# Exponents copied out of PSUM, one ScalarE Relu per block of w_out, GpSimd first at the shared port, first q and k loads in two parts

## The chip, the cores and the metric

The kernel runs on one core of one Trainium2 chip, as one program. The metric is the device time in microseconds, as the median of several runs; one more execution was recorded by the profiler. TensorE (PE) does the matrix products, ScalarE (ACT) the activations, VectorE (DVE) and GpSimd (POOL) elementwise work and reductions, and SyncE (SP) issues nearly all DMAs.

## The reference, cut to what matters

```python
# q, k, v: (4 batches, 8 heads, 576 positions, 64); w_in (512, 2048); w_out (2048, 512)
q_rot, k_rot = rotate(q), rotate(k)              # x*cos + swapped x*sin
scores = q_rot @ k_rot^T / sqrt(64)
attn = exp(scores - max(scores)); attn = attn / (sum(attn) + 1e-9)
x = (attn @ v), heads side by side               # 2304 tokens x 512
h = x @ w_in
g = h * tanh(softplus(h))                        # mish
out = g @ w_out
```

The weights w_in and w_out arrive as 64-bit floats; the kernel turns them into pairs of 16-bit halves (a high and a low part) with integer operations.

## The kernel before, in words

**Tiles.** Attention goes by pairs of heads (P = 0 to 15, four to a batch) and by five blocks of queries (t = 0 to 4). One step is: scores into PSUM (`psc`, L507 and L501), the negated row maximum on DVE (`mx`, L515), exp with a row sum on ACT (`e`, L517), the inverse of the sum on DVE (L526, L528). For the first batch (P below 4) the weights are then transposed on PE (L550 to L567) into `et`, copied out by ACT or DVE (L557, L558, L571 to L575), and multiplied with v (L645 to L648). For the others POOL or ACT makes the high half (`ew`, L532 or L534), DVE the low half (L538), and DMA transposes both. The multilayer part works on half a batch at a time: `h_unit` (L879, then Mish on ACT, L884), `h_split` into halves (`g`, L894 on ACT or L895 on DVE, then L898 on DVE), and `p_sub` (L915), which ends in an output.

**Rope.** Each head pair's q and k load is one DMA of 576 KB into `raw` (L405). Two multiplications by `cs` (L411) and two additions (L415), each over half of the 576 positions, follow on POOL or, in the first batch only, on DVE. A scaling of q by 0.125 on ACT closes it (L433).

**Weights.** A block's largest magnitude is found by DVE (L734, L378), crossed over the partitions by a PE transpose (L381) and a second reduction (L383), turned into an exponent (L371) and sent back to all partitions by a PE product with ones (L387); readers of the exponent read that PSUM bank. `decode` then takes each of four column blocks: ACT L775, a shift on POOL, ACT or DVE (L777 to L779), DVE L781 and L784, ACT L787, POOL L791. For w_out, `w2_decode` makes four scales at a time, one for each block of w_in: once a 128x4 `rel` (L831), and then for every block two more 128x4 operations (the two `ts` calls that make `s4`, both recorded as L371).

**Order.** The program states its operations in Python order with priorities; `Plan.order` plays them through with estimated durations and writes each engine's fixed list. Its rule for the port that DVE and POOL share: an operation whose entry has a fourth element may not start while the other engine runs one, and the two engines take turns (`turn`). ACT has two function tables, one for exp and one for Mish; a change of table costs `SWITCH` in the plan, and the plan keeps a table for at least `DWELL` ns. `SLOTS` says between which matmul groups of each half batch the attention steps go, `FRONT` how many steps go ahead of all; the `W` tables say at which step each weight block is loaded, scaled and decoded. Every engine works its list off in order and waits at each entry for what it reads.

Of the kernel before, what the change touches and what calls it, by code (L numbers as in the profile page):

```python
# [13 lines left out]
I32 = mybir.dt.int32  # L14
# [16 lines left out]
W1L = [2, 0, 1, 4]  # L31
W1S = [2, 3, 6, 7]
W1D = [5, 3, 7, 7]
VA = 4
W2L = [6, 8, 11, 9]
W2D = [10, 14, 14, 16]
PRE0 = 0
WSH = 10
FRONT = 11
TR = 107 / 128  # L40
ALPHA = 36
SLOTS = [
    [1, 8, 9, 12, 13, 17, 20, 21, 23, 27, 28, 31],
    [0, 2, 9, 10, 10, 11, 14, 15, 17, 17, 18, 19, 19, 20, 21, 25, 26, 26, 26, 31, 31],
    [8, 8],
    [5, 9, 10, 11, 12, 12, 15, 19, 20, 21, 22, 22, 22, 22, 25, 25, 26],
    [31],
    [0, 1, 2, 4, 9, 12, 12, 15, 16, 17, 18, 19, 22, 23, 23, 24, 24, 25, 25, 27, 28, 28, 30, 30],
    [],
    [1, 1, 2, 3, 4, 12, 18, 19, 21, 23, 24, 24, 24, 25, 28, 31],  # L50
]
AVL = 3
PREP = [5, 4, 0, 11]
PSH = [136, 39, 337]
ACTQ = ('out',)
QKB = 6
SWITCH = 1400
DWELL = 2251
PEN = 8
# [3 lines left out]
class Buf:  # L63


    def __init__(self, make, before=(), planned=True, of=None):
        self.planned, self.of = planned, of
        self.make, self.before, self.ops, self.state, self.ap = make, list(before), [], {}, None
        self.ring, self.slot = None, None
# [7 lines left out]
class Plan:  # L77
# [18 lines left out]
    def op(self, ways, w=(), r=(), table=None, after=()):  # L96
# [9 lines left out]
        for b, part in [x if isinstance(x, tuple) else (x, None) for x in r]:  # L106
# [23 lines left out]
    def order(self):  # L130
# [30 lines left out]
        port, turn = dict.fromkeys((DVE, POOL), 0.0), DVE  # L161
# [21 lines left out]
        while len(issued) < len(ops):  # L183
# [5 lines left out]
            for e in (PE, ACT, turn, POOL if turn == DVE else DVE, SP):  # L189
# [3 lines left out]
                while ready[e] or other:  # L193
# [49 lines left out]
                    else:  # L243
# [10 lines left out]
                        if len(ways[k]) > 3:  # L254
                            port[e], turn = end, POOL if e == DVE else DVE
# [61 lines left out]
def attention_mish_mlp(ctx: ExitStack, tc: tile.TileContext, qk, v, vflat, rope, ident_in, w_in, w_out, outT):  # L317
# [57 lines left out]
    def max_exponent(am, cols, lo, hi):  # L375
# [12 lines left out]
        return Buf(lambda: pb()[:, 0:1], planned=False, of=pb)  # L388
# [14 lines left out]
    def rope_turn(P, j, out=None):  # L403
        t = sbuf((128, 2, S), F32, "raw", 3)
        load("qk", dma_ns(128 * 2 * S * 4), lambda dma: dma(t(), qk[P][:, 2 * j:2 * j + 2]),  # L405
             w=[(t, 0), (t, 1), (t, 2), (t, 3)])
        for c in range(2):
            s = slice(c * HS, (c + 1) * HS)
# [4 lines left out]
            def add(e, s=s):  # L413
# [4 lines left out]
            op([(POOL, pool_ns(S), lambda f=mul: f(nc.gpsimd), 1), (DVE, dve_ns(S), lambda f=mul: f(nc.vector), 1)][:n],  # L418
               w=[(t, c), (t, 2 + c)], r=[cs])
            op([(POOL, pool_ns(HS), lambda f=add: f(nc.gpsimd), 1), (DVE, dve_ns(HS), lambda f=add: f(nc.vector), 1)][:n],  # L420
# [653 lines left out]
```

## Time and profile before

| what | value |
|---|---|
| median of 3 runs | 670.77 us (664.63, 670.91, 670.77) |
| the profiled execution | 662.89 us, span 661.1 us |
| mean granted TensorE clock | 0.968 |
| busy: PE, DVE, ACT, POOL | 599.6, 443.1, 455.6, 282.5 us |
| DMA | 82.50 MB, 125 GB/s over the span |
| ACT table loads | 66, of 1.283 us each |

PE is busy for 91% of the span, and the slices show where it is not: the first five, and a few after them. From about 200 us on most slices are full. A busy share is an average over stages; what bounds a stage is read from which wait ends last in it.

### The profile page before, as it was taken

Reading aid. Unit: us, or ns where it says so; the run is one execution under the profiler, and the core shown is the slowest. Engines: PE = TensorE matmul, PEld = TensorE weight load, DVE = VectorE, ACT = ScalarE, POOL = GpSimd, SP = SyncE. Lnnn points to the kernel's source line nnn. Section 1 sums busy time; section 2 is a strip of 40 time slices with the busy share of each in tenths; the row PEclk is TensorE's granted clock in tenths of the full one; section 3 lists DMA queues with packets and bytes.
Section 4 is the critical chain, followed back from the end, with each engine's and each line's share of the span. In section 5 each row is a group of like instructions: output and inputs, shape, how many; then the busy total and the mean of one; then the engine's idle time right before and its main releaser. Section 6 shows DMA issues by size and latency. Waiting matters only on the chain. (4 is left out here: it accounts for less than half of the span.)

```text
span 661.1 us, 13085 instructions
## 1 busy us (share of the span) xinstructions
PE 599.6 (91%) x5028; PEld 445.3 (67%) x5028; DVE 443.1 (67%) x961; ACT 455.6 (69%) x848; POOL 282.5 (43%) x264
## 2 busy tenths in 40 slices
PE   0576799889989998999999999999999999999997
PEld 0343455566668765678887677688877777887775
DVE  4998879998988888677776486875676576211210
ACT  2863979899889987488768776687869555623420
POOL 4795655666546876536362565460222010000000
PEclk9975978999989998999999999999999999999999
DMA  9961341452277765994667347663362376000000
GB/s 363 419 231 46 98 162 60 163 172 73 56 152 201 136 192 132 222 194 94 139 147 130 93 103 182 120 145 73 71 128 51 72 134 137 23 9 9 17 11 30
DMA packets 143534, 82.50 MB, mean 125 GB/s; under 512 B 129264, under 2 KB 133488, under 8 KB 141936
## 3 DMA queue, kind: packets, MB, share of 16 engines
q1 hardware_dynamic: 138864, 76.96, 46.9%
q10 hardware_dynamic: 4608, 4.72, 2.5%
q8 instruction: 39, 0.64, 0.4%
q14 instruction: 23, 0.19, 0.1%
HBM read 45.09 MB, written 4.72 MB: 75 GB/s over the span
## 5 line engine op out<-in xcount | busy, mean ns | idle before, releaser
L915 PE MATMUL bank<-g,w 128*128 128x256 f16 (+1 forms) x1536 | 201.9, 287 | 2.4 <-DVE g L898 1.2
L915 PEld LDWEIGHTS <-w 128*128 128x128 f16 x1536 | 146.9, 98 | 47.3 <-issue 10.5
L879 PEld LDWEIGHTS <-w 128*128 128x128 f16 x1536 | 148.8, 98 | 42.8 <-issue 6.2
L879 PE MATMUL bank<-xt,w 128*128 128x256 f16 (+1 forms) x1344 | 174.4, 286 | 2.5 <-DVE ew L575 0.8
L538 DVE SCALAR_TENSOR_TENSOR ew<-e,rs,ew 128x576 f16<-128x576 f32 x108 | 105.3, 997 | 27.8 <-POOL ew L532 18.2
L517 ACT ACTIVATE e<-psc,mx 128x576 f32<-128x576 f32 x144 | 105.7, 737 | 24.5 <-DVE mx L515 21.4
L532 POOL TENSOR_SCALAR ew<-e,rs 128x576 f16<-128x576 f32 x67 | 54.7, 824 | 157.9 <-DVE rs L528 99.7
L515 DVE TENSOR_REDUCE mx<-psc 128x1 f32<-128x576 f32 x144 | 103.4, 749 | 23.2 <-PE psc L507 19.7
L411 POOL TENSOR_TENSOR raw<-raw,cs 128x576 f32<-128x576 f32 x62 | 91.8, 1498 | 39.0 <-DMA raw<-in_qk 39.0
L898 DVE SCALAR_TENSOR_TENSOR g<-mh,cells,g 128x512 f16<-128x512 f32 (+1 forms) x64 | 58.2, 916 | 65.7 <-ACT g L894 65.7
L507 PE MATMUL psc<-qk 64*128 64x288 f32 (+1 forms) x736 | 86.9, 351 | 10.0 <-ACT e L517 7.1
L507 PEld LDWEIGHTS psc<-qk 64*128 64x128 f32 (+1 forms) x736 | 58.0, 189 | 32.3 <-ACT e L517 13.7
L884 ACT ACTIVATE mh<-bank,cells 128x256 f32<-128x256 f32 (+1 forms) x112 | 52.9, 500 | 32.3 <-PE bank L879 31.6
L791 POOL TENSOR_TENSOR w<-mr,w 128x512 f16<-128x512 f32 x30 | 35.9, 1201 | 40.7 <-ACT w L787 32.7
L534 ACT ACTIVATE ew<-e,rs 128x576 f16<-128x576 f32 x41 | 31.3, 774 | 26.6 <-DMA et<-ew 22.0
L526 DVE TENSOR_SCALAR sm<-sm 128x1 f32<-128x1 f32 x144 | 21.0, 149 | 37.0 <-ACT e L517 36.5
L894 ACT ACTIVATE g<-mh,cells 128x512 f16<-128x512 f32 (+1 forms) x55 | 42.5, 772 | 4.3 <-PE bank L915 3.3
L415 POOL TENSOR_TENSOR raw<-raw 128x288 f32<-128x288 f32 x48 | 44.6, 948 | 0.2
L517 ACT ACT_TABLE_LOAD x32 | 41.1, 1283 | 5.0 <-DVE mx L515 4.6
L884 ACT ACT_TABLE_LOAD x33 | 42.3, 1283 | 0.7
L923 ACT ACTIVATE ot<-bank,cells 128x256 f32<-128x256 f32 (+1 forms) x32 | 15.9, 496 | 37.1 <-PE bank L915 37.0
L657 PE MATMUL bank<-et,v 128*64 128x256 f16 (+1 forms) x288 | 40.8, 292 | 0.0
(104 smaller groups left out, 747.2 us busy)
## 6 DMA issues: line engine op xcount, KB each, us to landing
raw<-in_qk SPq DMA_DIRECT2D x32, 576.0 KB, 4.7
w<-in_w_in SPq DMA_DIRECT2D x4, 1024.0 KB, 12.4
stg<-in_v SPq DMA_DIRECT2D x12, 320.0 KB, 3.6
stg<-in_vflat SPq DMA_DIRECT2D x9, 384.0 KB, 3.5
w<-in_w_out SPq DMA_DIRECT2D x3, 1024.0 KB, 5.0
out_dram<-ot ACTq DMA_DIRECT2D x16, 160.0 KB, 2.4
g<-in_w_in SPq DMA_DIRECT2D x2, 1024.0 KB, 13.7
xt<-in_w_out SPq DMA_DIRECT2D x2, 1024.0 KB, 4.9
```

The source lines that it names most:

```text
L411: e.tensor_tensor(out=t()[:, :, s], in0=t()[:, :, s], in1=cs()[:, :, s], op=ALU.mult)
L415: e.tensor_tensor(out=to, in0=t()[:, 0, s], in1=t()[:, 1, s], op=ALU.add)
L507: nc.tensor.matmul(out, x[own, q], y[own, s], **kw)
L515: op((DVE, dve_ns(S), lambda: nc.vector.tensor_reduce(m(), pt()[:, :, :HS], axis=AX.XY, op=ALU.max, negate=True)), w=[m], r=[pt])
L517: op((ACT, act_ns(S, psum=True, ptr=2), lambda: nc.scalar.activation(e().rearrange("p (c s) -> p c s", c=2), pt()[:, :, :HS], AF.Exp, bias ...
L532: op([(POOL, 1.27 * S, lambda: nc.gpsimd.tensor_scalar(w()[:, c], e(), r()[:, h:h + 1], 1.0, op0=ALU.mult, op1=ALU.mult), 1), (ACT, act_ns ...
L538: op((DVE, dve_ns(S) + 61, lambda: nc.vector.scalar_tensor_tensor(out=w()[:, c], in0=e(), scalar=r()[:, h:h + 1], in1=w()[:, hc], op0=ALU. ...
L879: nc.tensor.matmul(hp(), w1()[:, wi, cc, f:f + 128], x()[:, xi, cc, q0:q0 + n], start=cc == 0 and a == 0, stop=cc == NCC - 1 and a == 2)
L884: op((ACT, act_ns(n, psum=True, ptr=1), lambda j=j, hp=hp: nc.scalar.activation(hn()[:, j, :n], hp(), AF.Mish, scale=uh())), w=[(hn, j)], ...
L894: op([(ACT, act_ns(2 * n, ptr=1), lambda: nc.scalar.activation(g()[:, 0, f, :n], hn()[:, :, :n], AF.Copy, scale=f32(gs))), (DVE, dve2_ns(2 ...
L898: op((DVE, dve_ns(2 * n) + 61, lambda: nc.vector.scalar_tensor_tensor(out=g()[:, 1, f, :n], in0=hn()[:, :, :n], scalar=f32(gs), in1=g()[:, ...
L915: nc.tensor.matmul(pp()[:, :n], w2e[e]()[:, wi, f], g()[:, gi, f % 8, :n], start=f == 0 and a == 0, stop=f == NF - 1 and a == 2)
```

## The change

- `max_exponent` now copies the exponent from the PSUM bank into an SBUF cell (one DVE COPY for each of 12 calls; 4 copies of w_in exponents that existed before are these now).
- `w2_decode`: the 128x4 `rel` and both 128x4 operations per block are gone. A 128x1 `rel`, a 128x1 bias per block, and one ACT Relu of 128x4 per block (4 in all) make the same scales.
- In the plan, POOL is always asked before DVE when the port is free; the turn-taking is gone.
- The rope constants and the loads of the first head pair come in two parts, 320 and 256 positions; for the first batch all rope work is cut at 320, the scaling of q follows each part, and the scores ask only for the part of q that they use (`QH`). The second part of q gets a later priority (`LATE`).
- `turned` takes banks only while another stays free; some duration estimates of the plan, `ALPHA`, `DWELL` (2251 to 308), `PEN`, `WSH`, the `W` tables, `PREP`, `PSH` and all of `SLOTS` are new, so that every engine's list is another.

Counted over the lists: ACT table loads 66 to 84; L894 on ACT 55 to 47 and its DVE form L895 9 to 17; L534 on ACT 41 to 34 and its POOL form L532 67 to 74; rope on DVE 2 multiplications and 3 additions to none. All matrix products are the same.

```diff
@@ -28,35 +28,38 @@
-W1L = [2, 0, 1, 4]
-W1S = [2, 3, 6, 7]
-W1D = [5, 3, 7, 7]
-VA = 4
-W2L = [6, 8, 11, 9]
-W2D = [10, 14, 14, 16]
+W1L = [0, 1, 2, 0]
+W1S = [0, 2, 2, 1]
+W1D = [6, 7, 8, 10]
+VA = 3
+W2L = [5, 3, 12, 14]
+W2D = [10, 15, 15, 17]
-WSH = 10
+WSH = 2
-ALPHA = 36
+ALPHA = 26
-    [1, 8, 9, 12, 13, 17, 20, 21, 23, 27, 28, 31],
+    [2, 8, 11, 12, 12, 18, 19, 21, 22, 23, 23, 26, 30],
...
-PREP = [5, 4, 0, 11]
-PSH = [136, 39, 337]
+LATE = 34
+PREP = [6, 4, 0, 11]
+PSH = [284, 1, 119]
+QH = [[0], [0], [0, 1], [1], [0, 1]]
+CUT = 320
-DWELL = 2251
-PEN = 8
+DWELL = 308
+PEN = 6
@@ -66,7 +69,7 @@
-        self.ring, self.slot = None, None
+        self.ring, self.slot, self.part = None, None, None
@@ -103,7 +106,7 @@
-        for b, part in [x if isinstance(x, tuple) else (x, None) for x in r]:
+        for b, part in [x if isinstance(x, tuple) else (x, x.part) for x in r]:
@@ -158,7 +161,7 @@
-        port, turn = dict.fromkeys((DVE, POOL), 0.0), DVE
+        port = dict.fromkeys((DVE, POOL), 0.0)
@@ -186,7 +189,7 @@
-            for e in (PE, ACT, turn, POOL if turn == DVE else DVE, SP):
+            for e in (PE, ACT, POOL, DVE, SP):
@@ -252,7 +255,7 @@
-                            port[e], turn = end, POOL if e == DVE else DVE
+                            port[e] = end
@@ -372,7 +375,7 @@
-    def max_exponent(am, cols, lo, hi):
+    def max_exponent(am, cols, lo, hi, out=None):
@@ -385,7 +388,10 @@
-        return Buf(lambda: pb()[:, 0:1], planned=False, of=pb)
+        got = small() if out is None else Buf(lambda: out[0]()[:, out[1]:out[1] + 1], of=out[0])
+        op((DVE, 70, lambda: nc.vector.tensor_copy(got(), pb()[:, 0:1])), w=[out or got], r=[pb])
+        got.part = out and out[1]
+        return got
@@ -400,12 +406,19 @@
-    def rope_turn(P, j, out=None):
+    def rope_turn(P, j, out=None, late=0):
-        load("qk", dma_ns(128 * 2 * S * 4), lambda dma: dma(t(), qk[P][:, 2 * j:2 * j + 2]),
-             w=[(t, 0), (t, 1), (t, 2), (t, 3)])
-        for c in range(2):
-            s = slice(c * HS, (c + 1) * HS)
+        halves = [slice(0, CUT), slice(CUT, S)] if P < NP else [slice(0, HS), slice(HS, S)]
+        if P == 0:
+            for c, s in enumerate(halves):
+                load("qk", dma_ns(256 * (s.stop - s.start) * 4), lambda dma, s=s: dma(t()[:, :, s], qk[P][:, 2 * j:2 * j + 2, s]),
+                     w=[(t, c), (t, 2 + c)])
+        else:
+            load("qk", dma_ns(128 * 2 * S * 4), lambda dma: dma(t(), qk[P][:, 2 * j:2 * j + 2]),
+                 w=[(t, 0), (t, 1), (t, 2), (t, 3)])
+        for c, s in enumerate(halves):
+            m = s.stop - s.start
+            plan.shift += late * c
@@ -415,10 +428,14 @@
-            op([(POOL, pool_ns(S), lambda f=mul: f(nc.gpsimd), 1), (DVE, dve_ns(S), lambda f=mul: f(nc.vector), 1)][:n],
-               w=[(t, c), (t, 2 + c)], r=[cs])
-            op([(POOL, pool_ns(HS), lambda f=add: f(nc.gpsimd), 1), (DVE, dve_ns(HS), lambda f=add: f(nc.vector), 1)][:n],
+            op([(POOL, pool_ns(2 * m), lambda f=mul: f(nc.gpsimd), 1), (DVE, dve_ns(2 * m), lambda f=mul: f(nc.vector), 1)][:n],
+               w=[(t, c), (t, 2 + c)], r=[(cs, c)] if P < NP else [(cs, 0), (cs, 1)])
+            op([(POOL, pool_ns(m), lambda f=add: f(nc.gpsimd), 1), (DVE, dve_ns(m), lambda f=add: f(nc.vector), 1)][:n],
+            if out is not None and j == 0:
+                op((ACT, act_ns(m), lambda s=s: nc.scalar.activation(out()[:, 0, s], out()[:, 0, s], AF.Copy, scale=0.125)),
+                   w=[(out, (0, c))])
+            plan.shift -= late * c
@@ -429,9 +446,7 @@
-            rope_turn(P, 0, z)
-            op((ACT, act_ns(S), lambda: nc.scalar.activation(z()[:, 0], z()[:, 0], AF.Copy, scale=0.125)),
-               w=[(z, (0, 0)), (z, (0, 1))])
+            rope_turn(P, 0, z, LATE)
@@ -486,7 +501,7 @@
-            terms, need, ns = (lambda: [(z()[:, 0], z()[:, 1])]), [(z, (j, c)) for j in range(2) for c in range(2)], 480
+            terms, need, ns = (lambda: [(z()[:, 0], z()[:, 1])]), [(z, (1, c)) for c in range(2)] + [(z, (0, c)) for c in QH[t]], 480
@@ -506,7 +521,7 @@
-        op((PE, 2 * ns + 100, fn), w=pts, r=need)
+        op((PE, 2 * ns + 300, fn), w=pts, r=need)
@@ -542,7 +557,7 @@
-            pt = bank()
+            pt = bank(1)
@@ -556,7 +571,7 @@
-        pt = bank()
+        pt = bank(1)
@@ -661,7 +676,7 @@
-            op((PE, 5 * pe_ns(3, n) + 220, fn), w=[po], r=[(V, 0), (V, 1)] + [(ET, x) for x in need])
+            op((PE, 5 * pe_ns(3, n) + 170, fn), w=[po], r=[(V, 0), (V, 1)] + [(ET, x) for x in need])
@@ -803,11 +818,10 @@
-        e = max_exponent(*st["w1", fq].amax(), 113.0, 142.0)
-        sc["w1s", fq], sc["w1u", fq] = pow2(e, -1, 143), pow2(e, 8, -897)
-        op((DVE, 70, lambda: nc.vector.tensor_copy(sc["w1e"]()[:, fq:fq + 1], e())), w=[(sc["w1e"], fq)], r=[e])
+        e = max_exponent(*st["w1", fq].amax(), 113.0, 142.0, (sc["w1e"], fq))
+        sc["w1s", fq], sc["w1u", fq] = pow2(e, -1, 143), pow2(e, 8, -897)
@@ -826,13 +840,13 @@
-            big, rel, all4 = small(), small((128, 4)), [(sc["w1e"], fq) for fq in range(4)]
+            big, all4 = small(), [(sc["w1e"], fq) for fq in range(4)]
-            tiny(rel, [big, *all4], lambda: nc.vector.tensor_scalar(
-                rel(), sc["w1e"](), big(), 143.0, op0=ALU.subtract, op1=ALU.add))
-            sc["w1rel"], sc["w1umax"] = rel, pow2(big, 8, -897)
-        s4 = ts(small((128, 4)), sc["w1rel"], e, 0.0, ALU.subtract, ALU.max)
-        s4 = ts(small((128, 4), I32), s4, BIT, None, ALU.mult)
+            sc["w1rel"], sc["w1umax"] = ts(small(), big, -1.0, 143.0, ALU.mult, ALU.add), pow2(big, 8, -897)
+        bias = ts(small(), sc["w1rel"], e, BIT, ALU.subtract, ALU.mult)
+        s4 = small((128, 4), I32)
+        op((ACT, 150, lambda: nc.scalar.activation(s4(), sc["w1e"](), AF.Relu, bias=bias(), scale=BIT)),
+           w=[s4], r=[bias] + [(sc["w1e"], fq) for fq in range(4)])
@@ -992,7 +1006,8 @@
-        op((SP, dma_ns(128 * 2 * S * 4), lambda: nc.sync.dma_start(cs(), rope)), w=[cs])
+        for c, s in enumerate((slice(0, CUT), slice(CUT, S))):
+            op((SP, dma_ns(256 * (s.stop - s.start) * 4), lambda s=s: nc.sync.dma_start(cs()[:, :, s], rope[:, :, s])), w=[(cs, c)])
```

**The first loads (SP) and POOL's first work.** SP before; `w_69` and the `g` tiles are homes of w_in blocks, the `raw` rows are k and q of pair 0, then of pair 1:

```order
L995 DMA cs<-in_rope 128x1152
L405 DMA raw<-in_qk 128x1152
L721 DMA w_69<-in_w_in 128x1024 x2
L405 DMA raw<-in_qk 128x1152
L996 DMA ident<-in_ident 128x128
L405 DMA raw<-in_qk 128x1152
L721 DMA g_94<-in_w_in 128x1024
L721 DMA g_96<-in_w_in 128x1024
L721 DMA w_69<-in_w_in 128x1024 x2
L405 DMA raw<-in_qk 128x1152
```

SP now:

```order
L1010 DMA cs<-in_rope 128x2x320
L414 DMA raw<-in_qk 128x2x320 x2
L1010 DMA cs<-in_rope 128x2x256
L414 DMA raw<-in_qk 128x2x256
L736 DMA g_91<-in_w_in 128x1024
L736 DMA g_93<-in_w_in 128x1024
L414 DMA raw<-in_qk 128x2x256
L417 DMA raw<-in_qk 128x1152
L1011 DMA ident<-in_ident 128x128
L736 DMA w_69<-in_w_in 128x1024 x4
L417 DMA raw<-in_qk 128x1152
```

k and the first 320 positions of q go ahead of all weights; the last `raw` row, q of pair 1, still has the same tiles ahead of it.

POOL before, from its first rope to q of pair 1 (the fourth L411 row):

```order
L411 TENSOR_TENSOR raw<-raw,cs 128x2x288
L415 TENSOR_TENSOR qk<-raw 128x288
L777 TENSOR_SCALAR w_69<-w_69 128x512 x2
L411 TENSOR_TENSOR raw<-raw,cs 128x2x288
L415 TENSOR_TENSOR qk<-raw 128x288
L411 TENSOR_TENSOR raw<-raw,cs 128x2x288 x2
L415 TENSOR_TENSOR qk<-raw 128x288 x2
L791 TENSOR_TENSOR w_68<-mr,w_68 128x512 x2
L777 TENSOR_SCALAR w_69<-w_69 128x512 x3
L791 TENSOR_TENSOR w_68<-mr,w_68 128x512
L411 TENSOR_TENSOR raw<-raw,cs 128x2x288 x2
L415 TENSOR_TENSOR qk<-raw 128x288 x2
```

POOL now, from k of pair 1 to q of pair 1 (L424 and L428 are the rope's lines, L792 the shift, L806 the low half of a decoded block):

```order
L424 TENSOR_TENSOR raw<-raw,cs 128x2x320
L424 TENSOR_TENSOR raw<-raw,cs 128x2x256
L428 TENSOR_TENSOR qk<-raw 128x320
L428 TENSOR_TENSOR qk<-raw 128x256
L792 TENSOR_SCALAR w_69<-w_69 128x512 x4
L806 TENSOR_TENSOR w_68<-mr,w_68 128x512
L792 TENSOR_SCALAR w_69<-w_69 128x512 x2
L806 TENSOR_TENSOR w_68<-mr,w_68 128x512
L424 TENSOR_TENSOR raw<-raw,cs 128x2x320
L424 TENSOR_TENSOR raw<-raw,cs 128x2x256
L428 TENSOR_TENSOR qk<-raw 128x320
L428 TENSOR_TENSOR qk<-raw 128x256
```

Both lists have L791 (now L806) entries ahead of q of pair 1; the block decoded first is now one that is scaled after the first scores.

**The w_out scales (DVE).** Before, around the one 128x4 `rel`:

```order
L526 TENSOR_SCALAR sm<-sm 128x1
L830 TENSOR_REDUCE cells<-cells 128x1
L575 COPY ew<-bank_74 128x128
L528 RECIPROCAL rs<-sm 128x1
L831 TENSOR_SCALAR cells<-cells 128x4
L558 COPY et<-bank_77 128x4x128
L526 TENSOR_SCALAR sm<-sm 128x1
L383 TENSOR_REDUCE cells<-bank_75 1x1
L528 RECIPROCAL rs<-sm 128x1
```

Now (L844 is the maximum that stood at L830, the two L374 after L386 are `rel` and the scale beside it):

```order
L543 RECIPROCAL rs<-sm 128x1
L844 TENSOR_REDUCE cells<-cells 128x1
L386 TENSOR_REDUCE cells<-bank_74 1x1
L374 TENSOR_SCALAR cells<-cells 128x1 x2
L374 TENSOR_SCALAR cells<-cells 1x1
L749 TENSOR_REDUCE cells<-qk 128x1
L530 TENSOR_REDUCE mx<-psc 128x1 x2
```

The 128x4 row has gone, and 128x1 rows stand in its place.

**Table changes (ACT), around the 115th exp.** Before:

```order
L517 ACT_TABLE_LOAD
L517 ACTIVATE e_5506,sm<-psc,mx 128x576
L517 ACTIVATE e_5534,sm<-psc,mx 128x576
L884 ACT_TABLE_LOAD
L884 ACTIVATE mh<-bank_74,cells 128x256
L884 ACTIVATE mh<-bank_77,cells 128x256
L894 ACTIVATE g_5456<-mh,cells 128x2x256
L884 ACTIVATE mh<-bank_75,cells 128x256
L884 ACTIVATE mh<-bank_74,cells 128x256
L894 ACTIVATE g_5456<-mh,cells 128x2x256
L438 ACTIVATE qk<-raw 128x576
L517 ACT_TABLE_LOAD
```

Now:

```order
L532 ACT_TABLE_LOAD
L532 ACTIVATE e_5535,sm<-psc,mx 128x576
L898 ACT_TABLE_LOAD
L898 ACTIVATE mh<-bank_77,cells 128x256
L898 ACTIVATE mh<-bank_76,cells 128x256
L532 ACT_TABLE_LOAD
L532 ACTIVATE e_5586,sm<-psc,mx 128x576
L898 ACT_TABLE_LOAD
L898 ACTIVATE mh<-bank_75,cells 128x256
L898 ACTIVATE mh<-bank_77,cells 128x256
L532 ACT_TABLE_LOAD
```

An exp pair that stood between two loads is now cut in places into single exps, with Mish between them.

## Rows read from the trace of the kernel before

**Rows 1.** Page, part 1: busy us of each engine, share of the span, instructions.

```profile
PE 599.6 (91%) x5028; PEld 445.3 (67%) x5028; DVE 443.1 (67%) x961; ACT 455.6 (69%) x848; POOL 282.5 (43%) x264
```

**Rows 2.** Busy us by stretch: PE, PEld, DVE, ACT, POOL; granted clock, DMA share, GB/s.

```profile
0.00:20.00 20.00, 3.25 (x11) 1.76 (x11) 11.18 (x20) 6.53 (x10) 11.71 (x16) 1.00 0.92 373
20.00:40.00 20.00, 13.31 (x71) 8.06 (x73) 18.23 (x49) 17.20 (x37) 16.40 (x16) 0.83 0.99 404
40.00:60.00 20.00, 11.81 (x65) 7.05 (x63) 19.24 (x41) 7.93 (x18) 14.41 (x15) 0.65 0.30 91
110.00:200.00 90.00, 79.21 (x667) 57.87 (x667) 81.05 (x194) 80.59 (x145) 50.15 (x46) 0.98 0.43 115
200.00:300.00 100.00, 94.56 (x816) 69.24 (x815) 78.91 (x178) 78.99 (x146) 64.26 (x54) 0.98 0.80 182
300.00:430.00 130.00, 126.69 (x1141) 97.33 (x1140) 92.75 (x178) 97.78 (x178) 66.65 (x59) 1.00 0.59 125
```

**Rows 3.** Timeline, the stall: start, us, engine, line, [idle before, releaser].

```profile
45.56 5.50 POOL L411 TENSOR_TENSOR raw<-raw,cs 128x576 f32<-128x576 f32 x4
...
47.01 7.43 DVE L831 TENSOR_SCALAR cells<-cells 128x4 f32<-128x4 f32 x1
...
51.00 1.16 POOL L791 TENSOR_TENSOR w<-mr,w 128x512 f16<-128x512 f32 x1
52.11 2.30 POOL L415 TENSOR_TENSOR qk<-raw 128x288 f32<-128x288 f32 x3
...
55.09 1.12 PE L550 MATMUL bank<-ident,e 128*128 128x128 f32 x4 [5.27 <-DVE sm L526]
...
62.54 0.42 DVE L676 TENSOR_TENSOR ew<-bank,ew 128x256 f32<-128x256 f32 x1 [2.81 <-PE bank L648]
```

**Rows 4.** Timeline: a 128x4 operation beside POOL; start, us, engine, line.

```profile
116.75 1.22 DVE L371 TENSOR_SCALAR cells<-cells,bank 128x4 f32<-128x4 f32 x1 [0.18 <-PE bank L387]
116.79 1.16 POOL L791 TENSOR_TENSOR w<-mr,w 128x512 f16<-128x512 f32 x1 [1.68 <-ACT w L787]
```

**Rows 5.** That line's instructions: min/median/max ns, first and last start.

```profile
L371 DVE TENSOR_SCALAR cells<-cells x45: 121/141/500, 14.1 to 295.6; 128x1 int32<-128x1 int32 x16, 1x1 int32<-1x1 int32 x12, 1x1 f32<-1x1 int32 x12, 128x4 int32<-128x4 f32 x4
...
L371 DVE TENSOR_SCALAR cells<-cells,bank x4: 227/1176/1252, 96.2 to 164.6; 128x4 f32<-128x4 f32 x4
```

**Rows 6.** Timeline, the start: first rope, first decode, scores of pairs 0 and 1.

```profile
5.94 0.76 DVE L411 TENSOR_TENSOR raw<-raw,cs 128x576 f32<-128x576 f32 x1 [4.96 <-DMA raw<-in_qk]
...
15.31 1.37 ACT L775 ACTIVATE bank<-w,cells 128x512 f32<-128x512 f32 x2 [2.88 <-DVE cells L371]
...
17.34 2.29 PE L507 MATMUL psc<-qk 64*128 64x288 f32 x8 [2.27 <-ACT qk L433]
...
28.36 1.16 POOL L791 TENSOR_TENSOR w<-mr,w 128x512 f16<-128x512 f32 x1 [2.43 <-ACT w L787]
...
34.83 2.29 PE L507 MATMUL psc<-qk 64*128 64x288 f32 x8 [0.53 <-ACT qk L433]
```

**Rows 7.** Groups by line: xcount, busy us, mean ns, idle before and its releaser.

```profile
L411 POOL TENSOR_TENSOR raw<-raw,cs 128x576 f32<-128x576 f32 x62 | 91.8, 1498 | 39.0 <-DMA raw<-in_qk 39.0
...
L415 DVE TENSOR_TENSOR qk<-raw 128x288 f32<-128x288 f32 x3 | 4.0, 1318 | 0.0
...
L810 DVE COPY cells<-bank 128x1 f32<-128x1 f32 x4 | 0.6, 144 | 0.0
...
L894 ACT ACTIVATE g<-mh,cells 128x512 f16<-128x512 f32 (+1 forms) x55 | 42.5, 772 | 4.3 <-PE bank L915 3.3
...
L517 ACT ACT_TABLE_LOAD x32 | 41.1, 1283 | 5.0 <-DVE mx L515 4.6
...
L534 ACT ACTIVATE ew<-e,rs 128x576 f16<-128x576 f32 x41 | 31.3, 774 | 26.6 <-DMA et<-ew 22.0 <-ACT e L517 3.4 <-DVE rs L528 1.0
```

**Rows 8.** PE's waits, 200 to 560 us: what for, us, times, longest.

```profile
PE psc L507 <- ACT e L517: 5.2, 10, 1.2
```

**Rows 9.** Low halves on DVE: min/median/max ns.

```profile
L538 DVE SCALAR_TENSOR_TENSOR ew<-e,rs,ew x108: 798/817/1967, 170.9 to 559.1; 128x576 f16<-128x576 f32 x108
```

## What the change should do to the time

> **What bounds the kernel now.** I read the busy times first: PE works 599.6 of 661.1 us [rows 1], so all that any order can gain lies in some 61 us of idle PE and in stretches of low clock. The table by stretches then says where these are [rows 2]. PE is idle for 16.8 us of the first 20, 6.7 of the next and 8.2 of the third, and the granted clock falls to 0.83 and 0.65 there; from 110 to 200 us it is idle for 10.8 of 90, from 200 to 300 for 5.4 of 100, from 300 to 430 for 3.3 of 130. The end is full. What PE waits for at the front is read from the engines beside it in the same rows: DVE is busy 18.23 and 19.24 of 20 us between 20 and 60, and 81.05 of 90 between 110 and 200, where ACT has 80.59. So until 200 us this is a kernel of DVE and ACT; later of PE.
>
> DVE's 19.24 us are not all work. In the timeline one operation on 128x4 numbers, L831, takes 7.43 us [rows 3]. It starts at 47.01, while POOL runs four multiplications from 45.56; POOL goes on with L791 and three additions without a gap until 54.41, and L831 ends at 54.44. PE's next transposes start after 5.27 us of waiting, released by the small DVE operation that had stood behind L831. Another 128x4 operation, at 116.75, takes 1.22 us, and one POOL operation lies over it, 116.79 to 117.95 [rows 4]. Operations of 128x1 on the same line stay at a median of 141 ns [rows 5]. So the multi-element form waits for POOL to run dry, and the one-element form doesn't.
>
> **The change part by part**, against the profiled execution's 662.89 us (1.8 us of it outside the span). It lies 1.2% below the median of 670.77, and I scale by that at the end.
>
> *The stall of L831.* The 128x4 operation becomes 128x1. Bounds: the whole 7.43 us, or nothing if the next DVE operation waited in its place. The PE wait that ended on it is 5.27 us, and a little is in the neighbours: I take -6.0.
>
> *What the stall did to the clock.* The stretch 40 to 60 us ran at 0.65 [rows 2], and after the stall DVE itself waited 2.81 us for PE's products with v [rows 3]. The granted mean says that most of that stretch was at 1.2 GHz and not 2.4, after PE had stood idle; half of that wait comes back. Between 0 and -2.8 us I take -1.5.
>
> *The later 128x4 operations.* Of the four with a PSUM operand the longest took 1.252 us and the median 1.176 [rows 5]; against the 0.227 of the shortest, three lose some 1.0 us each, 3.0 in all. Their stretch has DVE busy 90% and PE idle 12% [rows 2]. Between 0 and -3.0: -1.0.
>
> *Rope of the first batch off DVE.* Three additions of 1.318 us and two multiplications (no more than 1.5 us each, POOL's mean) leave DVE, about 5.5 us with their waiting [rows 7]; POOL takes them, some 5 us, in a stretch where it is busy 12 to 16 of 20 us [rows 2]. For a gain speaks that DVE is the fuller one; against it, that POOL's list now holds all rope of pairs 0 to 3. Bounds -3 and +3; -1.0.
>
> *First loads in two parts.* Now 960 KB (320 of 576 positions, three loads) are in front of the first scores' work, where 1152 KB had landed by 5.94 us [rows 6]. POOL then makes three multiplications and three additions: with 1.498 us [rows 7] and a third of 2.30 [rows 3] for 288 positions each, 4.7 + 2.4 = 7.1 us, so the first scores, at 17.34 before [rows 6], can start at about 13.5: -3.8. But the third scores, the first of pair 1, need q of pair 1, and the list of SP has the same nine megabytes ahead of it, at 373 and 404 GB/s [rows 2]: the queue can't be faster. And POOL reaches it behind two low halves of a decoded block. One such entry already waited 2.43 us for ACT before [rows 6]; the first decode, at 15.31 before [rows 6], now follows the second scores. So the third scores, at 34.83 before, may come 2 us later. Bounds -3.8 and +2.5; with DVE full from 20 us on I take 0. The extra DMAs (three on SP) are issued in front of weights that nobody wants before 18 us.
>
> *Copies of exponents.* Eight more at 144 ns [rows 7], and five one-element operations at 141 [rows 5]: 1.9 us of DVE, spread over 290 us, against banks that come free earlier. Bounds 0 and +1.9; +0.5.
>
> *Four Relu on ACT.* No row has one of 128x4; the nearest is a `g` half of 512 numbers a partition at 0.772 us [rows 7], so four cost ACT between 0 and 3.1 us. What hides them is ACT's idle time, 10% from 110 to 200 us [rows 2]; without that cover they would be paid in full. I take 0.
>
> *Eighteen more table loads.* At 1.283 us they are 23.1 us of ACT; eight `g` halves (0.772) go to DVE and seven `ew` (0.774) to POOL, 11.6 us, so ACT has 11.5 us more [rows 7]. The lists add nearly all of them behind the 74th of 144 exps, in the full stretches, where ACT is busy for 75% [rows 2]. In 360 us PE waited for exp in all 5.2 us, ten times [rows 8]. Half as many loads again in that wait would be 1 to 2 us; the bounds are 0 and +11.5; +1.2. *The Trainium skill, ScalarE: Activation LUTs, "What ACT_TABLE_LOAD costs", gives 1283 ns and as much again for a drain, 2.66 us for every switch; by it the loads would take 48 us of ACT. The trace agrees with the first number; the idle time before the exp loads is 5.0 us in all for 32 [rows 7], which leaves no room for a drain at each.*
>
> *POOL first in the plan.* The old rule lets DVE and POOL take turns; in the trace DVE got none through eight POOL operations [rows 3]. A list made with the true rule puts less DVE work behind a blocked operation. The low halves take 997 ns on the mean (105.3 us by 108), 817 in the median [rows 9]: 19 us of such waiting, most of it where PE is full. Bounds -6 and, for a list that is simply another, +4; -1.5.
>
> Sum: -6.0 - 1.5 - 1.0 - 1.0 + 0 + 0.5 + 0 + 1.2 - 1.5 = **-9.3 us**: 653.6 for a profiled execution. Times 670.77/662.89 that is 661.4; I say **661.5 us**, 1.4% faster. Within 1% is 664.1 to 677.5, and a difference of that size is about what a measurement of this kernel can tell from none.
>
> **Rivals.**
>
> *The front gives it back, 669 us.* POOL becomes what pair 1 to 3 wait for: third scores 2 us late, rope 3 us late, and of the 7.5 us of stall and clock only 5 arrive. -2 us. For it: POOL's order at the start, and that POOL waits for ACT in the middle of its list. Against it: POOL is less full than DVE.
>
> *The stall isn't the port's, 668 us.* The row shows 7.43 us under eight POOL operations on end. If DVE had got the port after the first of them, L831 would have ended near 48.4, and the rest would be another wait, which the 128x1 form in the same place inherits: -1.4 - 1.0 of the later ones, about -3. *The Trainium skill, SBUF — State Buffer, "SBUF: two separate sides", says that the pair of ports is held for one whole instruction and that the loser blocks until the first finishes; by that rule 1.4 us would be the most. The row at 116.75 agrees with it, the row at 47.01 differs.* I follow the longer row, since its end meets the end of POOL's run within 0.03 us.
>
> *Table loads come on the path, up to 683 us.* Exps now stand alone between two loads, so a step's second score bank comes free two loads and two Mish later. If this makes PE wait 1.283 us for each of 18 loads, that is 23.1 us in place of 1.2, and 662.89 - 10.5 + 23.1 = 675.5, or 683 against the median. It decides from 14 of the 18 loads on: then the time passes 677.5. For it: PE's only repeated late wait is on exp [rows 8]. Against: each is 1.2 us at most now, and ACT has a quarter of its time free.
>
> *All of DVE's relief counts, 654 us.* Removed from DVE are 7.4 + 3.0 + 5.5 + some 1.5 us, 17 in all, in stretches where it is full, and the first scores' 3.8 us stay: -17 us.
>
> **How the numbers follow.** Forecast 0.51 (its own range 657 to 666), front gives back 0.22, stall not the port's 0.05, table loads 0.10, all of the relief 0.12. Faster by over 1%: three quarters of the forecast, nearly all of the last case: 0.50, and a little of the second, 0.53. Slower by over 1%: the loads, 0.10. Within: 0.37. The range, 8 in 10, reaches from 652 (the full relief) to 671 (the front gives it all back); the loads' case and a better one than full relief are left out.
>
> **What would show it.** In the changed profile no DVE operation on `cells` should be over 0.3 us, and no DVE operation of 7 us; PE idle between 40 and 60 us should fall from 8.2 to about 3, with the clock above 0.8. First scores at 13 to 14 us, third at 33 to 37. 84 table loads, with PE's wait on exp after 200 us below 8 us. Wrong it would be if PE idles in the first 60 us as long as before (31.6 us [rows 2]), or if the wait on exp after 200 us is over 14 us.

## The result, and the profile after

The changed kernel takes 674.54 us (median of 19 runs, 669.06 to 679.07), the kernel before 666.26 in the same comparison. The ratio is **1.0112, 95% interval 1.0077 to 1.0147**: slower by 1.1%, some 7.5 us, where 1.4% faster was forecast. Ratios, here and below, leave out runs over 1.5% above the fastest of their kernel; for e1_ones and e12_rope_pool, where that is six of twelve and two of six, the ratio of the plain medians stands beside. The page of one execution, part 1, busy us:

```profile
PE 597.2 (89%) x5028; PEld 446.1 (67%) x5028; DVE 426.0 (64%) x967; ACT 469.6 (70%) x858; POOL 286.9 (43%) x278
```

Beside [rows 1], DVE has 17 us less to do and ACT 14 more; PE has 2.4 us less, and the span is 7.7 us longer (668.8). So PE idles 10 us more. By stretches, columns as in [rows 2]:

```profile
0.00:20.00 20.00, 6.09 (x22) 3.32 (x23) 6.38 (x15) 7.12 (x13) 13.69 (x19) 1.00 0.91 356
20.00:40.00 20.00, 10.85 (x65) 6.25 (x65) 17.97 (x48) 15.02 (x31) 17.14 (x18) 0.74 1.01 418
40.00:60.00 20.00, 16.16 (x106) 10.41 (x106) 18.50 (x64) 15.49 (x36) 18.13 (x19) 0.91 0.23 66
60.00:80.00 20.00, 10.99 (x68) 6.68 (x66) 16.51 (x30) 10.54 (x24) 15.87 (x16) 0.78 0.34 113
...
240.00:340.00 100.00, 84.22 (x743) 63.70 (x743) 64.65 (x166) 76.50 (x134) 49.10 (x47) 0.93 0.65 147
```

Two of these stretches in the kernel before:

```profile
60.00:80.00 20.00, 17.50 (x128) 10.81 (x124) 15.77 (x45) 15.01 (x36) 12.33 (x12) 0.93 0.26 83
...
240.00:340.00 100.00, 93.97 (x863) 72.80 (x861) 76.53 (x177) 70.52 (x137) 59.39 (x52) 0.98 0.71 154
```

Up to 60 us the forecast came true in the main: from 40 to 60 us PE idles 3.8 us in place of 8.2, at a clock of 0.91 in place of 0.65, and over the first 60 us 26.9 in place of 31.6 (from 20 to 40 us alone it idles 9.2 in place of 6.7). Then it is given back: 9.0 us idle from 60 to 80 us (before 2.5), and 15.8 from 240 to 340 (before 6.0). The timeline shows the first place; it starts with the scores that answer to [rows 6]:

```profile
12.57 2.29 PE L522 MATMUL psc<-qk 64*128 64x288 f32 x8 [12.57 <-ACT qk L436]
...
33.74 2.29 PE L522 MATMUL psc<-qk 64*128 64x288 f32 x8 [2.35 <-ACT qk L436]
...
69.13 1.22 DVE L749 TENSOR_REDUCE cells<-w 128x1 f32<-128x1024 f32 x1 [2.29 <-DMA w<-in_w_out]
...
71.25 2.76 POOL L424 TENSOR_TENSOR raw<-raw,cs 128x576 f32<-128x576 f32 x2
71.60 4.18 DVE L696 SCALAR_TENSOR_TENSOR xt<-ew,cells,xt 128x256 f16<-128x256 f32 x1
...
73.96 1.54 POOL L428 TENSOR_TENSOR raw<-raw 128x288 f32<-128x288 f32 x2
75.87 0.45 ACT L589 ACTIVATE ew<-bank 128x128 f32<-128x128 f32 x2 [5.48 <-DVE xt L696]
...
76.35 0.42 DVE L691 TENSOR_TENSOR ew<-bank,ew 128x256 f32<-128x256 f32 x1 [0.17 <-ACT ew L589]
...
76.83 1.12 PE L565 MATMUL bank<-ident,e 128*128 128x128 f32 x4 [8.50 <-DVE ew L691]
```

L831's stall [rows 3] is gone, but the low half of x, L696, which reads two operands in SBUF, stands for 4.18 us under an unbroken run of POOL and ends 0.28 us after it. ACT, DVE's product and PE's transposes wait behind it in turn. Two lines' instructions, min/median/max ns, the first answering to [rows 5]:

```profile
L374 DVE TENSOR_SCALAR cells<-cells x66: 121/142/215, 16.6 to 311.5; 128x1 int32<-128x1 f32 x21, 128x1 int32<-128x1 int32 x16, 1x1 int32<-1x1 int32 x12, 1x1 f32<-1x1 int32 x12
...
L696 DVE SCALAR_TENSOR_TENSOR xt<-ew,cells,xt x8: 469/540/4180, 71.6 to 165.8; 128x256 f16<-128x256 f32 x4, 128x320 f16<-128x320 f32 x4
```

Groups on ACT, and the low halves on DVE, columns as in [rows 7]:

```profile
L532 ACT ACT_TABLE_LOAD x41 | 52.6, 1283 | 4.6 <-DVE mx L530 3.8
...
L848 ACT ACTIVATE cells<-cells 128x4 int32<-128x4 f32 x4 | 1.2, 292 | 0.0
...
L898 ACT ACT_TABLE_LOAD x42 | 53.9, 1283 | 1.8 <-issue 0.7 <-ACT ot L937 0.4
...
L553 DVE SCALAR_TENSOR_TENSOR ew<-e,rs,ew 128x576 f16<-128x576 f32 x108 | 103.1, 981 | 30.8 <-POOL ew L547 26.0 <-ACT ew L549 4.5
```

PE's waits from 200 to 560 us, as in [rows 8]:

```profile
PE bank L893 <- ACT mh L898: 6.7, 3, 4.7
PE psc L522 <- ACT e L532: 5.2, 7, 1.7
PE bank L929 <- DVE g L912: 3.7, 1, 3.7
PE psc L516 <- ACT e L532: 3.3, 4, 1.7
```

The reader sees that no operation on `cells` stalls any more, that four Relu cost 1.2 us in all, and that the wait on exp is 8.5 us, hardly over the 8 that I had set. New are the waits on Mish and on `g`; before, the wait on exp stood alone at the head [rows 8].

### The profile page after: what moved, and what is told of

It reads as the page before. It is cut to its first block, busy times and chain, and to the rows that moved or that the text cites. A ratio compares the mean times of both kernels' runs of the same rounds, so it can differ in the third digit from the quotient of the medians.

```text
span 668.8 us, 13107 instructions
## 1 busy us (share of the span) xinstructions
PE 597.2 (89%) x5028; PEld 446.1 (67%) x5028; DVE 426.0 (64%) x967; ACT 469.6 (70%) x858; POOL 286.9 (43%) x278
## 4 chain that ended last, share of the span: by engine, by line
PE 41%; ACT 8%; DMA 7%; DVE 4%; issue 1%; POOL 0%; SPq 0%; ACTq 0%; DVEq 0%; POOLq 0%
PE bank L929 17%; PE bank L893 13%; DMA et<-ew 5%; PE psc L893 4%; PE psc L522 3%; PE bank L672 2%; ACT e L532 2%; ACT L898 2%; DVE ew L553 1%; ACT L532 1%; DMA stg<-in_v 1%; PE psc L516 1%; DVE g L912 1%; DVE mx L530 1%; ACT mh L898 1%
## 5 line engine op out<-in xcount | busy, mean ns | idle before, releaser
L929 PE MATMUL bank<-g,w 128*128 128x256 f16 (+1 forms) x1536 | 203.0, 289 | 3.7 <-DVE g L912 3.7
L893 PE MATMUL bank<-xt,w 128*128 128x256 f16 (+1 forms) x1344 | 177.0, 288 | 9.4 <-ACT mh L898 6.7
L893 PEld LDWEIGHTS <-w 128*128 128x128 f16 x1536 | 148.6, 98 | 52.7 <-issue 15.8
L929 PEld LDWEIGHTS <-w 128*128 128x128 f16 x1536 | 148.3, 99 | 48.3 <-issue 9.8
L547 POOL TENSOR_SCALAR ew<-e,rs 128x576 f16<-128x576 f32 x74 | 60.3, 821 | 200.1 <-DVE rs L543 84.7
L532 ACT ACTIVATE e<-psc,mx 128x576 f32<-128x576 f32 x144 | 105.6, 737 | 31.3 <-DVE mx L530 29.3
L553 DVE SCALAR_TENSOR_TENSOR ew<-e,rs,ew 128x576 f16<-128x576 f32 x108 | 103.1, 981 | 30.8 <-POOL ew L547 26.0
L530 DVE TENSOR_REDUCE mx<-psc 128x1 f32<-128x576 f32 x144 | 103.4, 749 | 18.2 <-PE psc L522 14.3
L522 PE MATMUL psc<-qk 64*128 64x288 f32 (+1 forms) x736 | 88.4, 350 | 27.5 <-ACT qk L436 14.9
L424 POOL TENSOR_TENSOR raw<-raw,cs 128x576 f32<-128x576 f32 (+2 forms) x64 | 91.1, 1440 | 27.4 <-DMA raw<-in_qk 27.2
L522 PEld LDWEIGHTS psc<-qk 64*128 64x128 f32 (+1 forms) x736 | 59.8, 189 | 50.9 <-ACT e L532 18.7
L898 ACT ACTIVATE mh<-bank,cells 128x256 f32<-128x256 f32 (+1 forms) x112 | 52.2, 499 | 25.8 <-PE bank L893 24.9
L806 POOL TENSOR_TENSOR w<-mr,w 128x512 f16<-128x512 f32 x32 | 37.6, 1183 | 23.9 <-ACT w L802 19.2
L549 ACT ACTIVATE ew<-e,rs 128x576 f16<-128x576 f32 x34 | 26.0, 772 | 29.8 <-DMA et<-ew 19.9
L428 POOL TENSOR_TENSOR raw<-raw 128x288 f32<-128x288 f32 x48 | 42.5, 907 | 0.1
L673 PE MATMUL bank<-et,v 128*64 128x256 f16 (+1 forms) x288 | 39.8, 288 | 0.0
L672 PE MATMUL bank<-et,v 128*64 128x256 f16 (+1 forms) x288 | 39.8, 288 | 0.0
L908 ACT ACTIVATE g<-mh,cells 128x640 f16<-128x640 f32 (+1 forms) x47 | 35.9, 774 | 2.8 <-PE bank L929 2.2
```

The lines of the kernel that those rows point to most:

```text
L424: e.tensor_tensor(out=t()[:, :, s], in0=t()[:, :, s], in1=cs()[:, :, s], op=ALU.mult)
L428: e.tensor_tensor(out=to, in0=t()[:, 0, s], in1=t()[:, 1, s], op=ALU.add)
L522: nc.tensor.matmul(out, x[own, q], y[own, s], **kw)
L530: op((DVE, dve_ns(S), lambda: nc.vector.tensor_reduce(m(), pt()[:, :, :HS], axis=AX.XY, op=ALU.max, negate=True)), w=[m], r=[pt])
L532: op((ACT, act_ns(S, psum=True, ptr=2), lambda: nc.scalar.activation(e().rearrange("p (c s) -> p c s", c=2), pt()[:, :, :HS], AF.Exp, bias ...
L547: op([(POOL, 1.27 * S, lambda: nc.gpsimd.tensor_scalar(w()[:, c], e(), r()[:, h:h + 1], 1.0, op0=ALU.mult, op1=ALU.mult), 1), (ACT, act_ns ...
```

## The experiments

Every ratio is to the kernel before, run on the same chip (medians 664.8 to 666.7); 1% is 6.7 us. Differences to e1_ones are given as a range, by the medians and by the ratios. In those that keep a list, the planner's order is taken as it is and single entries are moved or split behind it, since a planner that is asked again writes another list.

**The stall alone (e1_ones).**

```diff
-            tiny(rel, [big, *all4], lambda: nc.vector.tensor_scalar(
-                rel(), sc["w1e"](), big(), 143.0, op0=ALU.subtract, op1=ALU.add))
+            tiny(rel, [big, *all4], lambda: [nc.vector.tensor_scalar(
+                rel()[:, i:i + 1], sc["w1e"]()[:, i:i + 1], big(), 143.0, op0=ALU.subtract, op1=ALU.add) for i in range(4)])
```

(and the two operations on `s4` alike). 

> The kernel before, its list of instructions kept in order, with one thing changed: each DVE operation on 128x4 numbers (L831 and the two on the scales of a w_out block) becomes four on 128x1. Theory A (the stall of L831 is the port's, and in this list no later DVE operation with two SBUF inputs stands under the same run of GpSimd): no DVE operation over 3 us between 40 and 62 us, PE idle between 40 and 60 us falls from 8.2 to about 3, and the time falls by 4 to 8 us, ratio to before 0.988 to 0.994. Rival B (the stall is made good later, since DVE then only waits for PE or ACT): ratio 0.998 to 1.002. Rival C (the next DVE operation inherits the stall): a DVE operation of 5 us or more still stands in 47 to 55 us, ratio about 1.00.

Measured: 660.54 us, **0.9851 (0.9808 to 0.9893)**; by the medians 0.991. So it is 6 to 10 us faster. Its timeline:

```profile
47.67 0.55 DVE L831 TENSOR_SCALAR cells<-cells 128x1 f32<-128x1 f32 x4
...
55.04 1.16 POOL L791 TENSOR_TENSOR w<-mr,w 128x512 f16<-128x512 f32 x1
55.09 4.14 DVE L415 TENSOR_TENSOR qk<-raw 128x288 f32<-128x288 f32 x1
56.15 2.76 POOL L411 TENSOR_TENSOR raw<-raw,cs 128x576 f32<-128x576 f32 x2
```

Its stretches, columns as in [rows 2]:

```profile
40.00:60.00 20.00, 15.02 (x105) 9.10 (x102) 18.38 (x52) 9.62 (x22) 18.91 (x18) 0.90 0.29 92
60.00:80.00 20.00, 16.61 (x97) 10.31 (x97) 14.85 (x44) 15.77 (x37) 10.63 (x11) 0.74 0.26 83
...
240.00:340.00 100.00, 92.96 (x853) 72.29 (x851) 76.00 (x177) 69.00 (x135) 58.65 (x53) 0.98 0.73 155
```

The stall is gone and half handed on: the next DVE operation with two operands in SBUF, L415, takes 4.14 us until POOL's run ends. Yet PE idles 5.0 us there in place of 8.2, at a clock of 0.90. Theory A's price came (0.991 lies in its range, 0.9851 is a little better), though a DVE operation of over 3 us still stands; C is seen in the row and is not what the time goes by. The recorded execution took 662.16 us, only 0.7 less than that of before, so its rows show where the stall went and not the whole of the 6 to 10 us. This version beats both kernels.

**The inherited stall (e9_rope_behind).** In the list of after:

```diff
+        late = [i for i, (n, k) in enumerate(todo) if n in (804, 805, 806, 807)]   # rope of pair 4, POOL
+        stop = next(i for i, (n, k) in enumerate(todo) if n == 403)                # a low half, L806
...
+        todo[stop + 1:stop + 1] = [todo[i] for i in late]
...
```

> The kernel after, its list kept but for four entries of GpSimd (two multiplications and two additions of rope for pair 4, at 71.25 to 75.50 us) that move behind the next two low halves of the decoded blocks, so that no GpSimd operation stands at the port while DVE makes the two low halves of x (L696). Theory A (the stall moved from L831 to L696): the two take about 0.5 us each instead of 0.4 and 4.2, PE's wait of 8.50 us on L691 falls to 4 to 5 us, and the ratio to before is 1.004 to 1.007 instead of 1.011. Rival B (that wait is set by the late block of w_out and not by the port): PE's wait stays at 8 us, ratio 1.011 as of the kernel after.

Measured: 668.69 us, 1.004 (1.0006 to 1.0073). The two L696 (here L703) in the timeline:

```profile
72.00 0.87 DVE L703 SCALAR_TENSOR_TENSOR xt<-ew,cells,xt 128x256 f16<-128x256 f32 x2
```

PE's wait behind them in the first 120 us (L691 is L698 here; us, times, longest):

```profile
PE bank L572 <- DVE ew L698: 4.4, 1, 4.4
```

As theory A had it: the pair took 4.58 us in the kernel after (4.18 and 0.47, a little overlapped) and takes 0.87, the wait goes from 8.50 to 4.4. Between the two ratios lie 0.7%, 4.8 us, with 1.6 to 8.0 by their intervals. The rest of that wait begins with a late block of w_out, for which DVE stands until 69.54 us; this is read from the rows and was not tried.

**Half of the change (e2_code, e3_tables), and other lists (e14_nudge, e6_first).**

```diff
 e2_code:   the code of after; LATE, SLOTS, ALPHA, DWELL, PEN, W*, PREP, PSH of before
 e3_tables: the code of before; those numbers of after
 e14_nudge: the kernel before with
-ALPHA = 36
+ALPHA = 35
 e6_first:  the kernel before with
-            for e in (PE, ACT, turn, POOL if turn == DVE else DVE, SP):
+            for e in (PE, ACT, POOL, DVE, SP):
```

> The code of the kernel after with the tables of the kernel before (the planner's numbers and the slots; no late term). Theory A (the loss of the change comes from its tables, which make another list and 18 more table loads): ratio to before 0.985 to 0.997, 66 table loads as before. Rival B (the edits of the code lose by themselves, by the rope of the first batch on GpSimd and by GpSimd first): ratio 1.008 or more.

> The code of the kernel before with the tables of the kernel after. Theory A (the tables lose by themselves): ratio to before 1.010 to 1.025, with PE idle for over 12 us between 240 and 340 us. Rival B (they lose only with the new code): ratio 0.995 to 1.005.

> The kernel before with one number of its planner moved by one step (ALPHA 35 in place of 36), the rest of its tables and its code kept: what a list that is simply another costs. Theory A (the tables are fitted to one list, and any other is some per cent slower, as with the two halves of the change taken alone): ratio to before 1.01 to 1.04. Rival B (such a nudge costs nothing, and the halves lose by what they do): ratio 0.997 to 1.003.

> The kernel before with one of the planner's rules changed, GpSimd always ahead of DVE at the port in place of turns; tables and code as before. Theory A (any list that the tables aren't fitted to loses 1.5 to 4%, whatever the rule): ratio to before 1.015 to 1.04, as e14_nudge. Rival B (the rule gains by itself, as the prediction took it, 1.5 us): ratio 0.99 to 1.00.

Measured: e2_code 690.88 us, 1.0367 (1.0324 to 1.0409); e3_tables 697.10 us, 1.0467 (1.0417 to 1.0518); e14_nudge 678.48 us, 1.0194 (1.0134 to 1.0254); e6_first 690.42 us, 1.0374 (1.0312 to 1.0436). My theory of e2, that the code gains and the tables lose, fell: each half alone loses three to four times what both lose together, e3 more than its theory A had. And one step of one number costs 13 us, though the matrix products are the same. The table loads are not: before's list has 66, and these four, in their order, have 80, 94, 88 and 82, against what theory A of e2 had (66). The loads of e14_nudge (one more stands at its start):

```profile
L884 ACT ACT_TABLE_LOAD x44 | 56.5, 1283 | 1.5 <-ACT ot L923 0.8
...
L517 ACT ACT_TABLE_LOAD x43 | 55.2, 1283 | 6.1 <-DVE mx L515 5.4
```

At 1.283 us each, the 14 to 28 more are 18 to 36 us of ACT. That is less than the loss in e2 and e6 and more than it in e3 and e14, so loads don't set the loss one for one; what part of it they are isn't shown. So neither half has a price of its own: a list made anew was 2 to 5% slower in all four. That before's numbers fit before's list and hardly any other is the likely reading; it rests on these four lists.

**The rope, nearly alone (e12_rope_pool).** In e1_ones:

```diff
+            k = 0 if ways[0][0] == POOL and ways[k][0] == DVE else k
```

> e1_ones (before's list, 128x1 forms) with the five rope operations of the first batch that DVE had made by GpSimd instead, at the same place of the list: the term of the prediction for the rope by itself. Theory A (it relieves DVE, and the 4.14 us of L415 at 55.09 go): ratio to before 0.978 to 0.985, below that of e1_ones. Rival B (GpSimd becomes what the scores of pairs 1 to 3 wait for): above that of e1_ones, 0.988 to 0.995.

The edit moves whatever GpSimd could take and DVE had: beside the five of the rope, one shift of a block of w_in and two low halves of decoded blocks.

Measured: 661.48 us, 0.9881 (0.9821 to 0.994), by the medians 0.992. That is 0.3% above e1_ones by the ratios, with 0.4 and 0.6% to either side in their intervals: no difference that can be told. L415's 4.14 us on DVE go and no gain can be told.

**Eighteen loads more (e13_loads), and fewer (e15_joined, e16_ones_joined).**

```diff
 e13_loads, in e1_ones, behind 9 of the exps:
+    plan.extra = lambda: nc.scalar.activation(spare, ones()[0:1, 0:1], AF.Mish)
 e15_joined, e16_ones_joined: exp | Mish | exp  ->  exp | exp | Mish, with what depends on that Mish behind it
+        todo = self.joined(todo, 9, 60)     # in e11_ew_behind
+        self.joined(self.order(), 5, 60)    # in e1_ones
```

> e1_ones with nine extra Mish of one number, each between two exps that stood under one table load, at nine places spread evenly behind the 74th exp: 18 more table loads, 84 in all as in the kernel after, and nothing else. Theory A (the loads lie in ScalarE's free time there): 1 to 4 us more than e1_ones, ratio to before 0.986 to 0.991. Rival B (each comes on the path): 18 times 1.283 us, 20 us or more, ratio to before 1.015 or more.

> e11_ew_behind with nine exps of its list moved ahead of the one to three Mish that stood between them and the exp before, so that each shares the table load of that exp: 18 table loads fewer, 66 in all as in the kernel before, with the rest of the list of the kernel after kept. Theory A (what e13_loads cost, 1.3 us for each load, is what the change pays too): 15 to 25 us less than e11_ew_behind, ratio to before 0.965 to 0.98. Rival B (the list of after is fitted to its loads: PE has Mish's products to do meanwhile, and a Mish that comes later costs what a load saves): ratio 0.995 to 1.010.

> e1_ones with five exps of its list moved ahead of the Mish between them and the exp before in the same way: 10 table loads fewer, 56 in all. Theory A (a load taken away gives back its 1.28 us): 8 to 13 us less than e1_ones, ratio to before 0.966 to 0.975. Rival B (PE then waits for the later Mish instead): ratio 0.985 to 1.000.

Measured: e13_loads 679.32 us, 1.02 (1.0151 to 1.0248), 19 to 23 us above e1_ones: 18 times 1.283 is 23.1, and the nine Mish add 0.2 us each. e15_joined 681.29 us, 1.025 (1.0201 to 1.0299), 15 us *above* e11_ew_behind. e16_ones_joined 684.68 us, 1.0292 (1.0248 to 1.0337), 26 to 29 us above e1_ones. Both are slower than either of their theories had. PE's longest wait after 200 us in e1_ones:

```profile
PE psc L507 <- ACT e L517: 7.7, 15, 1.2
```

The same in e13_loads:

```profile
PE psc L515 <- ACT e L525: 17.5, 15, 3.3
```

After 120 us, PE's waits on Mish in e11_ew_behind:

```profile
PE bank L905 <- ACT mh L910: 1.7, 5, 0.5
```

PE's longest wait after 120 us in e15_joined:

```profile
PE bank L948 <- ACT mh L953: 15.2, 9, 4.8
```

PE's waits on Mish after 120 us in e1_ones:

```profile
PE bank L645 <- ACT mh L887: 1.1, 1, 1.1
...
PE bank L550 <- ACT mh L887: 0.7, 1, 0.7
```

And the two longest in e16_ones_joined:

```profile
PE bank L924 <- ACT mh L929: 15.6, 3, 6.9
PE bank L687 <- ACT mh L929: 5.4, 1, 5.4
```

The loads put into a finished list cost nearly their whole time, some 10 us of it in PE's wait on exp; ACT's free time does not cover it, against my theory. Loads taken out of one in this way don't give it back: the Mish behind them comes later, and PE waits for that. But e15 moves Mish and loads at once, so it doesn't price the loads of after. At e13's price its 18 would be 19 to 23 us, more than all it lost. Against that, PE waits for exp little longer in after (8.5 us) than in e1_ones (8.1, counting a second row of 0.4), and that wait is where e13 paid (17.5). Whether loads are a part of its loss, by way of the Mish that they put off, stays open. *The Trainium skill, ScalarE: Activation LUTs, "What ACT_TABLE_LOAD costs", has 2.66 us for a switch, which would make 48 us of the 18; e13_loads measured 19 to 23 in all.*

**The waits from 240 to 340 us (e11_ew_behind, e17_low_behind).**

```diff
 e11_ew_behind, in the list of e9: `ew` on ACT behind g, exp, g
+        for n, behind in ((1136, 1143), (1257, 1271), (1333, 1433)):
 e17_low_behind, in that of e11: the low halves of `g` ahead of those of `ew` on DVE
+        for n in (1142, 1144):
+            j = next(i for i, x in enumerate(todo) if x[0] == 1138)
```

> e9_rope_behind with three more entries moved, all of ScalarE: three multiplications that make `ew` (L549 of the kernel after, at 240.62, 282.02 and 297.65 us) and that waited 3.27, 1.96 and 3.37 us for a turning DMA to free their buffer, move behind the exps and the Mish that stood after them in ScalarE's list. Theory A (after 240 us the list of after loses since Mish and exp stand behind such a wait): PE's waits of 3.66 us at 249.92 and 4.67 us at 300.27 shrink below 1.5 us each, PE idle from 240 to 340 us falls from 14 to 16 us to 8 to 10, and the ratio to before goes from 1.004 to 0.992 to 0.998. Rival B (PE is bound there by the turning DMAs, so the wait only changes its name): ratio 1.002 to 1.006.

> e11_ew_behind with two more entries moved: on DVE the two low halves of `g` (L912 of the kernel after) go ahead of the two low halves of `ew` that in e11 took 0.89 us of waiting for ScalarE and 2.11 us of work in front of them, while PE waited 4.93 us for `g`. Theory A (a wait on the buffers of `ew` only passes from ScalarE's list to DVE's, and PE waits behind either): PE's wait on L912 near 248 us falls from 4.9 to about 1.5, PE idle from 240 to 340 us from 13.4 to about 10, the time by 2 to 4 us, ratio to before 0.997 to 1.000. Rival B (PE then waits as long for the scores or the turned weights that come later): ratio 1.001 to 1.005.

Measured: e11_ew_behind 666.88 us, 1.0022 (0.999 to 1.0054); e17_low_behind 666.86 us, 1.0042 (1.0007 to 1.0077). PE's longest waits from 236 to 345 us in e11_ew_behind (L941 is L929, L534 is L522):

```profile
PE bank L941 <- DVE g L924: 4.9, 1, 4.9
PE psc L534 <- ACT e L544: 4.0, 5, 1.8
```

And in e17_low_behind (L533 is L516, L539 is L522, L946 is L929):

```profile
PE psc L533 <- ACT e L549: 5.7, 2, 4.0
PE psc L539 <- ACT e L549: 3.9, 4, 2.0
PE bank L946 <- DVE g L929: 1.7, 2, 1.5
```

e11 took away PE's wait of 4.67 us on Mish and left that on `g`, now behind DVE's low halves of `ew`; e17 took away that one, and PE waited 4.03 us for an exp at 247.75. PE idles 13.4 and 14.3 us from 240 to 340 us; in e9_rope_behind, from which they start, it is 13.9. Rival B of both: the wait changes its name.

## Why the prediction was wrong, by its steps

**The stall, the clock, the later 128x4 operations: -8.5 us.** Right as a sum. In before's list they gave 6 to 10 us (e1_ones), which doesn't part them; of the clock, e1_ones has 0.90 for 0.65 from 40 to 60 us and 0.74 for 0.93 in the next 20. The reading behind it, that the 128x4 form "waits for POOL to run dry", is too wide: it did at 47.01 us, and one of the later four did not (last section).

**The stall's heir.** I had it as the lower bound of the first term ("nothing if the next DVE operation waited in its place") and in a rival at 0.05, there only for the 128x1 form, which does not stall; I never looked for which operation it would be. The heirs are other lines and forms: L415 in e1_ones, L696 after the change. *By the rule of the Trainium skill, SBUF — State Buffer, "SBUF: two separate sides", that the loser blocks until the first instruction finishes, L696 could have waited for one multiplication of 1.4 us; it took 4.18, as L831 had taken 7.43, and two rows in the last section agree with the rule.* By e9_rope_behind, the stall of L696 cost 4.8 us (1.6 to 8.0) of the 7.5 by which the time rose.

**Rope off DVE, -1.0.** e12_rope_pool, with three operations more, could tell no gain. **First loads, 0.** The first scores came 4.8 us earlier and the third 1.1; this is gone by 40 us, when PE has worked 16.9 us in place of 16.6. **Copies +0.5 and Relu 0.** 1.2 us of ACT for Relu; not tried apart.

**Table loads +1.2, and the plan -1.5 with +4 as the end "for a list that is simply another".** Here it failed, by the plan's term above all. Between e1_ones and after lie 14 us by the medians and 17 by the ratios, where these terms and the rope, loads and copies had -0.8 in all. I priced the new list by the operations that it adds and the waits that it loses, as if the rest would stay; but the rest is another list. The lists of e14 and e6 show +13 and +25 us where I had +4, and e6 is the rule by itself, which I had as a gain. The ground of that gain hardly moved: the low halves took 981 ns on the mean in the kernel after, where I had 997. (The 105.3 us that I set beside the 997 count overlapping time once; by 108 they are 975.) The rival of the table loads named a price that e13_loads confirms in e1_ones's list, about 1.283 us each; that the list of after pays it is neither shown nor excluded.

What stays open: of the 14 to 17 us, L696 is shown for about 5. The cause of the other 10 or so is not settled by an experiment; table loads and the order of Mish, exp and `ew` are both in it and were not parted. The rows put some 9 of it to 240 to 340 us, where PE idles 15.8 us against 7.0 in e1_ones, but two repairs there only renamed the wait. Whether numbers searched for e1_ones's code would gain more wasn't tried.

What I said would prove it wrong looked at the first 60 us and at exp, and neither sign came (26.9 us idle, 8.5 us of wait); the loss was in the 20 us after that stretch and, by the rows, in waits on Mish and `g` from 240 us on.

## What to carry to other kernels

Where a planner writes the order, take one edit in the old order first, by splitting or moving entries behind the planner: here that gave 1 to 1.5%, which the full change turned into a loss. A new list must be priced as a new list, and its error bar taken from a list that differs by as little as possible (one number by one step: 2% here, with 22 table loads more), before any term of it is believed. When a stall at a shared port goes, name the next operation that needs the port under the same run, whatever its form.

## What the runs showed that I had not expected

Three DVE operations got the port they share with POOL only when POOL's whole unbroken run was over, and not after its next instruction: 4.18 us for L696 (ended 0.28 us after POOL), 4.14 for L415 in e1_ones (0.32 after), 7.43 for L831 (0.03 after) [rows 3]. L831 stood as long again in e14_nudge (7.43) and 4.29 us in e6_first. It is no rule of the port, though. In the trace of before, others were let in after one instruction while POOL's run went on:

```profile
164.40 1.41 POOL L411 TENSOR_TENSOR raw<-raw,cs 128x576 f32<-128x576 f32 x1
164.58 1.25 DVE L371 TENSOR_SCALAR cells<-cells,bank 128x4 f32<-128x4 f32 x1
165.77 3.51 POOL L415 TENSOR_TENSOR raw<-raw 128x288 f32<-128x288 f32 x4
...
436.47 2.79 POOL L411 TENSOR_TENSOR raw<-raw,cs 128x576 f32<-128x576 f32 x2 [0.45 <-DMA raw<-in_qk]
437.88 1.93 DVE L898 SCALAR_TENSOR_TENSOR g<-mh,cells,g 128x512 f16<-128x512 f32 x1
439.22 1.24 POOL L415 TENSOR_TENSOR raw<-raw 128x288 f32<-128x288 f32 x1
```

L371, of 128x4 as L831 but with one operand in PSUM, ends at 165.83, as POOL's multiplication does, and POOL goes on to 169.28. L898, with two operands in SBUF as L696, ends at 439.81, and it is POOL's next addition that takes longer, 1.24 us where three took 2.30 [rows 3]. What decides between the two is open.

ACT, which in e1_ones is busy for 454.8 of 660.4 us, hid next to nothing of 18 loads.
